# Unscaled exponentials in batch 0 and a scheduler whose ties are broken by random numbers, in an attention and channel-mixing kernel

## The chip, the core and the metric

The kernel runs on one core of one Trainium2 chip. The metric is the time of one execution in device microseconds (us). The engines are TensorE (PE in the profile; its weight loads are PEld), VectorE (DVE), ScalarE (ACT), GpSimd (POOL) and SyncE (SP), which issues nearly all DMAs. Each engine takes its instructions in the order in which the program wrote them for it, and they wait for each other by semaphores.

## The reference

Eight batches of 12 heads, 448 tokens, head size 64. Attention with an RMS norm of q and k, then a channel mix on its output:

```python
q_n, k_n = (rmsnorm(q, g_q), rmsnorm(k, g_k))
scores = scale * np.matmul(q_n, k_n.transpose(0, 1, 3, 2))
scores = scores - np.max(scores, axis=-1, keepdims=True)
attn = np.exp(scores)
attn = attn / (np.sum(attn, axis=-1, keepdims=True) + 1e-09)
out = np.matmul(attn, v)
...
xk = mu_k * x + (1.0 - mu_k) * x_prev
xr = mu_r * x + (1.0 - mu_r) * x_prev
k = np.maximum(xk @ w_k, 0.0)
v = k * k @ w_v
r = 1.0 / (1.0 + np.exp(-(xr @ w_r)))
return r * v
```

`x` is the attention's output with the heads side by side (768 columns), and `x_prev` the same, one token later. The three weights are float64 in the input (768 x 1024, 1024 x 768, 768 x 768).

## The kernel before

**Tiles.** Four heads of one batch are a quad `u` (24 in all, three to a batch), two heads a pair `i` (48, six to a batch). `load` fetches a quad's q and k, `stats` and `preps` normalise them, and `turn` or a transposing DMA brings them into the layout of the score products (`stk`). A quad has seven groups of score products (the list `groups`, line 824): three for the first pair, one shared by both pairs, three for the second. `scores` (826) issues a group's products into two PSUM banks; `expo` (864) reduces the row maximum on DVE and takes the exponential on ACT, which also sums the rows; `probs` (876) takes the probabilities further. `vload` and `vprep` (764) fetch and scale V; its small matmul of `vs` with the identity finds the maximum over partitions. `attends` (947) multiplies a pair's transposed probabilities (`pT`) with V into one PSUM bank `av` and copies it to the tile `x`. `mixk`, `mixr` and `mix` (1001) make xk and xr from `x`. `weights` (1037), `wscale` and `wsplit` turn the float64 weights into two f16 halves; a product of a weight tile with itself finds its column norms. `moe` (1144) does the products of a batch: eight tiles of xk with `wk`, and then, for each block of tokens and each half of the columns, xr with `wr` (1193) and the squared result `kk` with `wv`. Every product in f16 halves is three matmuls, so a batch has 144 matmuls xk with wk, 126 xr with wr and 168 kk with wv.

**Batch 0 is different.** Its three quads (`u < U32`, `U32 = 3`) work in float32. Their probabilities aren't transposed by a DMA, as in the other batches, but on PE, in `probs_pe` (909): two small DVE instructions make the scaled reciprocals of the row sums, two POOL passes multiply the exponentials by them (128x448 each), then seven transposes by the identity go to PSUM, and ACT or DVE copies them to `pT`. Ahead of 130 us PE also does the preparation of the weights, and much of the time it multiplies identity by identity in bf16: fillers, of which below.

**What sets the order.** Each of these functions is a thread that yields operations; the class `Plan` keeps a modelled clock for each engine and decides which thread's next operation is written next. `run` (365) computes for each thread the time at which its operation could start (the later of its engine's clock and the end of what it reads), takes off a tenth of the thread's priority, and takes the least (line 380):

```python
k = max(self.clk[th[2][0].eng] + wait, th[3] + slack) - PS * (th[1]() if callable(th[1]) else th[1])
```

`emit` (292) writes the operation behind the last one of its engine (so every instruction of the trace has its line, 298) and moves the modelled clock on, for PE by a cost in the operation's `form`: 130 ns a transpose (`TR_COST`), 110 ns a matmul of the weights' norms. Where the model sees PE idle by more than 200 ns ahead of an operation of certain kinds, `warm` (350) puts in fillers, 57 ns each, for 80% of that gap. So the number of fillers at a place tells how long a gap the planner foresaw there.

**The banks.** Eight PSUM banks go round among the users; `attends` and `vprep` share two of them (`OT_SHARE`).

Of the kernel before, what the change touches and what calls it, by code (L numbers as in the profile page):

```python
# [1 line left out]

# [14 lines left out]
P = 128  # L17
HD = 64
# [61 lines left out]
V_POOL = True  # L80
PE_T = 6
AHEAD = 0
U32 = 3
# [12 lines left out]
SC_KEEP = 1  # L96
TR_COST = 130
W_GAP = 6e3
# [122 lines left out]


WARM = ("tr", "sc", "t6", "av", "moe")
WARM_GAP = 200
# [5 lines left out]
class Plan:  # L230
    LAT = 35

    def __init__(self, tc):
        self.tc = tc
        self.clk = dict.fromkeys(("PE", "DVE", "ACT", "POOL", "SP"), 0.0)
        self.last, self.use, self.threads = {}, {}, []
        self.form, self.dma_free, self.acc, self.n = None, {"SP": 0.0, "ACT": 0.0}, False, 0
        self.held = {"DVE": [], "POOL": []}
        self.filler, self.own, self.bank, self.awake, self.warm_at = None, None, {}, False, 0.0

    def margin(self, form):
# [12 lines left out]
    def spawn(self, gen, prio=0):  # L254
        th = [gen, prio, None, 0.0]
        self.threads.append(th)
        self.advance(th)
# [14 lines left out]
    def advance(self, th):  # L272
        try:
            x = next(th[0])
        except StopIteration:
            self.threads.remove(th)
            return
        if isinstance(x, Op):
            x = [x]
        th[2] = x  # L280
        th[3] = self.ready(x) if isinstance(x, list) else 0.0

# [82 lines left out]
    def run(self):  # L365
        while self.threads:
            best, key = None, None
            for th in list(self.threads):
# [9 lines left out]
                if self.acc and th[2][0].eng == "ACT" and th[2][0].kw.get("accum_out") is not None:  # L378
                    wait += ACC_GAP
                k = max(self.clk[th[2][0].eng] + wait, th[3] + slack) - PS * (th[1]() if callable(th[1]) else th[1])  # L380
                if best is None or k < key:
# [101 lines left out]
def attn_moe_kernel(tc, q, k, v, small_in, w_k, w_v, w_r, out):  # L483
# [41 lines left out]
    st = {"wdone": 0, "g": 0, "moe": 0, "vl": 0, "gm": False, "mus": False, "want": "xk", "sg": 0, "su": 0, "pu": 0, "vi": 0, "wkeys": 0, "kdone": 0, "zq": 0, "tq": 0, "lu": 0, "pz": 0}  # L525
    LD, SS, VF, VV, TQ, PT, BS, BSC, XT, XK, XKN, XR, CNT, OS, CARRY, FR = {}, {}, {}, {}, {}, {}, {}, {}, {}, {}, {}, {}, {}, {}, {}, {}

# [180 lines left out]
    def turn(w, X, n, u):  # L708
        for a0 in range(0, NT, 4):
# [5 lines left out]
            for a in range(m):  # L715
# [4 lines left out]
                ops.append(T.transpose(form=("tr", TR_COST), out=o, in_=w[:, a0 + a, :], identity=ident))  # L720
            ops[0].form = ("tr", TR_COST * m)
            yield ops
# [100 lines left out]

    groups = [(u, *g) for u in range(NQ) for g in ((0, 0), (0, 2), (0, 4), (0, NT - 1), (1, 0), (1, 2), (1, 4))]

# [38 lines left out]
    def expo(gi, j, both, sums, D, tp):  # L864
        sp = both[j]
        if tp is not None:
            yield V.tensor_reduce(out=sums[:, j:j + 1], in_=sp[:, 0:S], axis=AX.X, op=ALU.max, negate=True)
            yield A.activation(out=tp.bitcast(F32).rearrange("p a c -> p (a c)")[:, j * S:(j + 1) * S], in_=sp[:, 0:S], func=AF.Exp, bias=sums[:, j:j + 1], accum_out=sums[:, 4 + 2 * j:5 + 2 * j])
            banks["sc"].put(sp)
            D[j] = True  # L870
            return
        yield V.tensor_reduce(out=sums[:, j:j + 1], in_=sp[:, 0:S], axis=AX.X, op=ALU.max, negate=True)
        yield A.activation(out=sp[:, 0:S], in_=sp[:, 0:S], func=AF.Exp, bias=sums[:, j:j + 1], accum_out=both[0][:, S + j:S + j + 1])
        D[j] = True
# [34 lines left out]
    def probs_pe(u, x, t0, sums, tp):  # L909
        r = sums[:, 8:11:2]  # L910
        yield V.tensor_scalar(out=r, in0=sums[:, 4:7:2], scalar1=1e-9, scalar2=2.0 ** -15, op0=ALU.add, op1=ALU.mult)
        yield V.reciprocal(out=r, in_=r)
        tf = tp.bitcast(F32).rearrange("p a c -> p (a c)")
        for j in range(2):
            w = tf[:, j * S:(j + 1) * S]
            yield G_.tensor_scalar(out=w, in0=w, scalar1=r[:, j:j + 1], scalar2=0.0, op0=ALU.mult, op1=ALU.add)
        c0 = S - HD if t0 == NT - 1 else x * S + (t0 + x) * HD
        for a0 in range(0, NT, 4):
# [3 lines left out]
            st["zq"] -= 1  # L922
            yield [T.transpose(form=("tr", TR_COST * m), out=z[:, a * P:(a + 1) * P], in_=tf[:, (a0 + a) * P:(a0 + a + 1) * P], identity=ident) for a in range(m)]
            src = z[:, 0:m * P].rearrange("p (a c) -> p a c", c=P)
# [22 lines left out]
    def attends():  # L947
        for i in range(NPAIR):
# [3 lines left out]
            pT = PT.pop(i)  # L952
            av = yield from banks["ot"].get()
            ops = []
            passes = PASSES32 if vl is None else PASSES
# [15 lines left out]
            for lo, hi in ((0, NT),) if i % 2 == 0 else ((NT - 1, NT), (0, NT - 1)):  # L971
                o = 0 if i % 2 == 0 or lo else HD
                yield A.activation(out=x[:, 1 + lo:1 + hi, :].rearrange("p t c -> p (t c)"), in_=av[:, o:o + (hi - lo) * HD], func=AF.Copy, scale=1.0 if iv is None else iv)
            banks["ot"].put(av)
# [62 lines left out]
    def weights():  # L1037
        for nm, w, kt, c, ci in WT:
# [27 lines left out]
            w16 = f.bitcast(BF16).rearrange("p (i n two) -> p i n two", two=2, n=P)[:, :, :, 1]  # L1066
            yield [T.matmul(form=("w", 110 * kt), out=pg[:, c % nb * P:(c % nb + 1) * P], lhsT=w16[:, i, :], rhs=w16[:, i, :], start=(c == 0 and i == 0), stop=(last and i == kt - 1)) for i in range(kt)]
            plan.filler = None if last else T.matmul(form=("x", 0), out=pg[:, 3 * P:4 * P], lhsT=ident16, rhs=ident16, start=False, stop=False)
# [241 lines left out]
```

## Time and profile before

| what | value |
|---|---|
| median of 3 runs | 989.4 us (989.07 to 989.49) |
| the profiled execution, time | 990.39 us |
| the profiled execution, span from the first to the last instruction | 988.6 us |
| PE, DVE, ACT, POOL busy, share of the span | 94%, 67%, 79%, 68% |
| mean granted clock of PE | 0.984 |
| instructions | 18862 |

A row of a group of instructions reads: line, engine, operation, output<-inputs by the program's names, partitions x elements, count | busy time in us, mean duration of one in ns | idle time of the engine just before them, and what ended most of it. A row of the waits reads: engine, tile and line that waited <- engine, tile and line waited for: us in total, times, the longest. A row of the timeline reads: start in us, duration in us, engine, operation, and in brackets the idle time before it and what ended it. `nat`, `xk` and `natx` are buffers that hold a group's exponentials (`xk` is lent out for that in batch 0), `sums` the row sums, `ps` any PSUM bank, `ident` the identity.

### The profile page before, as it was taken

The numbers are of one execution on the slowest core, as the hardware profiler recorded it, in microseconds if no ns is written. First come the engines' busy times: TensorE is split into PE (matmuls) and PEld (weight loads), VectorE is DVE, ScalarE is ACT, GpSimd is POOL, SyncE is SP. The second block draws the span as 40 slices with busy tenths as digits, with TensorE's granted clock in tenths as the row PEclk, the third lists the DMA queues.
The fourth block names the chain that finished last, engine by engine and source line by source line (L and its number), as shares of the span: only waits on it lengthen the run. The fifth ranks groups of instructions, "written<-read, shape, count | busy, mean of one in ns | idle before, by whom it ended". The sixth has DMA issues, their size and how long they took to land. (4 is left out here: it accounts for less than half of the span.)

```text
span 988.6 us, 18862 instructions
## 1 busy us (share of the span) xinstructions
PE 926.8 (94%) x6408; PEld 494.9 (50%) x6408; DVE 663.1 (67%) x1815; ACT 781.6 (79%) x1741; POOL 676.5 (68%) x744
## 2 busy tenths in 40 slices
PE   6878789799898999989999999999999999999997
PEld 5545454455444555445445454445544555565564
DVE  7888976888675878758778888688867875011000
ACT  4788899788996899979999999999999977424200
POOL 2789799756797677877787765977798725525400
PEclk9999999799898999999999999999999999999999
DMA  6634584789957999789979999899986993100000
GB/s 245 195 111 155 181 218 98 146 173 206 211 117 168 203 225 214 150 168 221 188 163 190 237 187 235 168 187 198 235 178 138 204 202 78 22 17 33 1 32 32
DMA packets 357648, 156.43 MB, mean 158 GB/s; under 512 B 336432, under 2 KB 336560, under 8 KB 357552
## 3 DMA queue, kind: packets, MB, share of 16 engines
q1 hardware_dynamic: 357408, 154.78, 71.5%
q8 instruction: 50, 0.82, 0.3%
q10 hardware_dynamic: 144, 0.46, 0.1%
q14 instruction: 46, 0.38, 0.1%
HBM read 60.24 MB, written 11.01 MB: 72 GB/s over the span
## 5 line engine op out<-in xcount | busy, mean ns | idle before, releaser
L298 PE MATMUL ps<-wv,kk 128*128 128x384 f16 x1344 | 234.4, 326 | 3.8 <-POOL kk L298 1.9
L298 PE MATMUL ps<-xk,wk 128*128 128x448 f16 x1152 | 225.9, 353 | 1.7 <-DVE o L298 1.0
L298 ACT ACTIVATE ps<-ps,sums 128x448 f32<-128x448 f32 x294 | 187.1, 638 | 20.9 <-DVE sums L298 19.2
L298 DVE TENSOR_REDUCE sums<-ps 128x1 f32<-128x448 f32 x336 | 192.4, 616 | 13.2 <-PE ps L298 12.5
L298 PE MATMUL ps<-wr,xr 128*128 128x384 f16 x1008 | 181.8, 332 | 3.3 <-ACT x L298 2.8
L298 DVE SCALAR_TENSOR_TENSOR nat<-ps,sums,nat 128x448 f16<-128x448 f32 x240 | 157.6, 678 | 35.6 <-ACT nat L298 34.8
L298 ACT ACTIVATE nat<-ps,sums 128x448 f16<-128x448 f32 (+1 forms) x272 | 171.2, 673 | 12.4 <-DVE sums L298 6.1
L298 PEld LDWEIGHTS <-kk 128*128 128x128 f16 (+1 forms) x1350 | 128.0, 98 | 100.9 <-issue 17.4
L298 PEld LDWEIGHTS <-wk 128*128 128x128 f16 (+1 forms) x1194 | 112.8, 98 | 112.6 <-issue 14.6
L298 PE MATMUL ps<-stk 64*128 64x448 f16 (+3 forms) x1104 | 128.2, 377 | 14.8 <-DVE nat L298 4.1
L298 PEld LDWEIGHTS <-xr 128*128 128x128 f16 x1008 | 97.4, 99 | 77.8 <-issue 18.6
L298 DVE SCALAR_TENSOR_TENSOR o<-o,ps 128x384 f32<-128x384 f32 x56 | 30.7, 549 | 111.9 <-PE ps L298 111.9
L298 DVE SCALAR_TENSOR_TENSOR df<-x,bsc,ps 128x448 f32<-128x448 f32 x96 | 64.4, 676 | 56.6 <-ACT ps L298 47.0
L298 PE MATMUL ps<-pT,vh 128*64 128x448 f16 x588 | 94.3, 364 | 3.8 <-DMA pT<-natx 1.3
L298 ACT ACTIVATE o<-ps,bsc 128x384 f32<-128x384 f32 x48 | 29.4, 612 | 72.0 <-PE ps L298 72.0
L298 POOL TENSOR_TENSOR qk<-qk,ss 128x896 f32<-128x896 f32 x36 | 60.8, 1688 | 23.3 <-DVE ss L298 22.8
L298 PEld LDWEIGHTS <-stk 64*128 64x128 f16 x1008 | 35.2, 97 | 69.8 <-issue 43.8
L298 POOL TENSOR_SCALAR o<-o,bsc 128x768 f32<-128x768 f32 x24 | 21.7, 905 | 67.7 <-DVE o L298 52.6
L298 POOL TENSOR_TENSOR xr<-df,xr 128x448 f16<-128x448 f32 x48 | 49.4, 1037 | 25.9 <-ACT xr L298 25.7
L298 POOL TENSOR_SCALAR vf<-vf,bstat 128x896 f32<-128x896 f32 x42 | 42.6, 1014 | 33.7 <-DVE bstat L298 28.7
L298 ACT ACTIVATE ps<-x,bsc 128x448 f32<-128x448 f32 x96 | 63.2, 668 | 2.1 <-POOL bsc L298 1.8
L298 POOL TENSOR_TENSOR xk<-df,xk 128x448 f16<-128x448 f32 x48 | 49.6, 1036 | 21.6 <-ACT xk L298 21.4
(174 smaller groups left out, 1576.6 us busy)
## 6 DMA issues: line engine op xcount, KB each, us to landing
vf<-in_v_dram SPq DMA_DIRECT2D x42, 448.0 KB, 4.2
out_dram<-o SPq DMA_DIRECT2D x28, 384.0 KB, 3.1
qk<-in_k_dram SPq DMA_DIRECT2D x23, 448.0 KB, 4.5
qk<-in_q_dram SPq DMA_DIRECT2D x22, 448.0 KB, 4.4
raw<-in_moe_w_v_dram SPq DMA_DIRECT2D x12, 512.0 KB, 4.3
raw<-in_moe_w_r_dram SPq DMA_DIRECT2D x12, 384.0 KB, 3.2
kk<-in_moe_w_k_dram SPq DMA_DIRECT2D x8, 384.0 KB, 5.1
raw<-in_moe_w_k_dram SPq DMA_DIRECT2D x8, 384.0 KB, 3.1
```

The source lines that it names most:

```text
L298: r = op.fn(op.kw["out"], op.kw["value"]) if op.fn.__name__ == "memset" else op.fn(**op.kw)
```

## The change

Three things are changed.

First, in batch 0 the exponentials are transposed unscaled. `expo` lets ACT put the row sums into a tile `acc` that is kept for the quad, 14 columns. `probs_pe` leaves out the two DVE instructions and the two POOL passes. In `attends` a pair's eight columns of `acc` become scaled reciprocals `rr` (two DVE instructions); the new function `spread_rows` multiplies each column, repeated 64 times, with the identity on PE, so that the reciprocals of all tokens stand in the bank `av` in the layout of the output (eight float32 matmuls); ACT copies them to `x`; then the products with V go into the same bank; and DVE multiplies `av` with the copied factors, where ACT copied `av` before.

Second, the planner's costs for transposes and for the weights' norms are others, and the spreading matmuls have a cost.

Third, `run` adds a random number to each candidate's key. It is drawn when the operation is made ready, is uniform between 0 and one of five amplitudes (3 to 200 ns of the modelled time), and its generator is seeded anew in each 15 us of the modelled time. The list `SEEDS` has one seed per stretch, 62 in all, 12 of them 0, which means no noise; a seed's remainder by 5 chooses the amplitude. The diff's core:

```diff
+PE_ROW = 125
...
-TR_COST = 130
+TR_COST = 109
...
+AMPS = [3.0, 10.0, 30.0, 80.0, 200.0]
+SEG = 15e3
...
+        self.seg = -1
+
+    def noise(self):
+        g = int(self.now() / SEG)
+        seed = SEEDS[g] if g < len(SEEDS) else 0
+        if g != self.seg:
+            self.seg, self.rng = g, Random(seed)
+        return AMPS[seed % 5] * self.rng.random() if seed else 0.0
...
+        th[4] = self.noise()
...
-                k = max(self.clk[th[2][0].eng] + wait, th[3] + slack) - PS * (th[1]() if callable(th[1]) else th[1])
+                k = max(self.clk[th[2][0].eng] + wait, th[3] + slack) - PS * (th[1]() if callable(th[1]) else th[1]) + th[4]
...
-            ops[0].form = ("tr", TR_COST * m)
+            ops[0].form = ("tr", TR_COST * m + 45)
...
+    QUAD = ((0, 0), (0, 2), (0, 4), (0, NT - 1), (1, 0), (1, 2), (1, 4))
+    groups = [(u, *g) for u in range(NQ) for g in QUAD]
+
+    def spread_rows(pt, x, col):
+        ops = []
+        for g, (y, t0) in enumerate(QUAD):
+            if t0 == NT - 1:
+                rows, cols = slice(x * HD, (x + 1) * HD), slice(x * (S - HD), x * (S - HD) + HD)
+                cols = slice(0, HD) if x else slice(S - HD, S)
+            elif y == x:
+                rows, cols = slice(0, P), slice((t0 + x) * HD, (t0 + x + 2) * HD)
+            else:
+                continue
+            for h in range(2):
+                ops.append(T.matmul(form=("f", 0), out=pt[h * HD:(h + 1) * HD, cols], lhsT=col(g)[rows, h:h + 1].broadcast_to([rows.stop - rows.start, HD]), rhs=ident[rows, rows], start=True, stop=True))
+        ops[0].form = ("f", PE_ROW * len(ops))
+        return ops
...
+            u = groups[gi][0]
+            if u < U32:
+                if u not in AC:
+                    AC[u] = small.tile([P, 2 * NT], F32, name="acc", bufs=U32)
+                c = 2 * (gi % NT) + j
+                acc = AC[u][:, c:c + 1]
+            else:
+                acc = sums[:, 4 + 2 * j:5 + 2 * j]
             yield V.tensor_reduce(out=sums[:, j:j + 1], in_=sp[:, 0:S], axis=AX.X, op=ALU.max, negate=True)
-            yield A.activation(out=tp.bitcast(F32).rearrange("p a c -> p (a c)")[:, j * S:(j + 1) * S], in_=sp[:, 0:S], func=AF.Exp, bias=sums[:, j:j + 1], accum_out=sums[:, 4 + 2 * j:5 + 2 * j])
+            yield A.activation(out=tp.bitcast(F32).rearrange("p a c -> p (a c)")[:, j * S:(j + 1) * S], in_=sp[:, 0:S], func=AF.Exp, bias=sums[:, j:j + 1], accum_out=acc)
...
-        r = sums[:, 8:11:2]
-        yield V.tensor_scalar(out=r, in0=sums[:, 4:7:2], scalar1=1e-9, scalar2=2.0 ** -15, op0=ALU.add, op1=ALU.mult)
-        yield V.reciprocal(out=r, in_=r)
         tf = tp.bitcast(F32).rearrange("p a c -> p (a c)")
-        for j in range(2):
+        if u >= U32:
+            r = sums[:, 8:11:2]
+            yield V.tensor_scalar(out=r, in0=sums[:, 4:7:2], scalar1=1e-9, scalar2=2.0 ** -15, op0=ALU.add, op1=ALU.mult)
+            yield V.reciprocal(out=r, in_=r)
+        for j in range(2) if u >= U32 else ():
             w = tf[:, j * S:(j + 1) * S]
             yield G_.tensor_scalar(out=w, in0=w, scalar1=r[:, j:j + 1], scalar2=0.0, op0=ALU.mult, op1=ALU.add)
...
+            u = i // 2
+            xc = x[:, 1:, :].rearrange("p t c -> p (t c)")
+            if u < U32:
+                o = 6 * (i % 2)
+                rr = small.tile([P, 8], F32, name="rr", bufs=2)
+                yield V.tensor_scalar(out=rr, in0=AC[u][:, o:o + 8], scalar1=1e-9, scalar2=2.0 ** -15, op0=ALU.add, op1=ALU.mult)
+                yield V.reciprocal(out=rr, in_=rr)
+                yield spread_rows(av, i % 2, lambda g: rr[:, 2 * g - o:2 * g - o + 2])
+                yield A.copy(out=xc, in_=av[:, 0:S]) if i % 2 == 0 else A.copy(out=x[:, NT:, :], in_=av[:, 0:HD])
+                if i % 2:
+                    yield A.copy(out=x[:, 1:NT, :], in_=av[:, HD:S])
...
-                yield A.activation(out=x[:, 1 + lo:1 + hi, :].rearrange("p t c -> p (t c)"), in_=av[:, o:o + (hi - lo) * HD], func=AF.Copy, scale=1.0 if iv is None else iv)
+                if u < U32:
+                    xs = xc[:, lo * HD:hi * HD]
+                    yield V.tensor_tensor(out=xs, in0=av[:, o:o + (hi - lo) * HD], in1=xs, op=ALU.mult)
+                    continue
+                yield A.activation(out=x[:, 1 + lo:1 + hi, :].rearrange("p t c -> p (t c)"), in_=av[:, o:o + (hi - lo) * HD], func=AF.Copy, scale=iv)
...
-            yield [T.matmul(form=("w", 110 * kt), out=pg[:, c % nb * P:(c % nb + 1) * P], lhsT=w16[:, i, :], rhs=w16[:, i, :], start=(c == 0 and i == 0), stop=(last and i == kt - 1)) for i in range(kt)]
+            yield [T.matmul(form=("w", 57 * kt + 20), out=pg[:, c % nb * P:(c % nb + 1) * P], lhsT=w16[:, i, :], rhs=w16[:, i, :], start=(c == 0 and i == 0), stop=(last and i == kt - 1)) for i in range(kt)]
```

**How it moves instructions.** On PE, fillers ahead of the first product xk with wk go from 346 to 279; the last product with V of batch 0 and that first product are parted by 118 fillers before and 38 now. Three places follow, of the order before and of the one now. In the rows a number behind a name is a buffer's.

The first is POOL in batch 0, where the last tile of `wk` is decoded (`kk` and `wr` from `raw`) and the first is scaled by `WSC`, rows 52 to 57 of POOL before:

```order
L298 TENSOR_SCALAR kk_98<-raw_705 128x384
L298 TENSOR_TENSOR nat_822<-nat_822 128x14x32
L298 TENSOR_SCALAR kk_98<-raw_753 128x384
L298 TENSOR_SCALAR xk_99<-xk_99,sums_103 128x448 x2
L298 TENSOR_SCALAR wr<-raw_885 128x384
L298 TENSOR_SCALAR wk<-wk,WSC 128x768
```

The two passes with `sums` are a group's scaling. On POOL at the same place, rows 38 to 42, stands now:

```order
L314 TENSOR_SCALAR kk_98<-raw_728 128x384
L314 TENSOR_SCALAR kk_98<-raw_749 128x384
L314 TENSOR_TENSOR nat_956<-qk_520,ss 128x2x7x64
L314 TENSOR_SCALAR wr<-raw_882 128x384
L314 TENSOR_SCALAR wk<-wk,WSC 128x768
```

The scaling is gone, the place comes 15 rows earlier, and the normalising of a later quad (`qk` with `ss`) has come in between.

The second is ACT where the last pair of batch 0 is taken out of PSUM (`x_1574` before, `x_1543` now; `x` with `bsc` is the mix, `wr` a weight's split, `ps` from `raw` a weight's decoding). Before:

```order
L298 ACTIVATE ps_1584<-raw_1542 128x512
L298 ACTIVATE wr<-wr,WSC 128x768
L298 ACTIVATE x_1574<-ps_1575 128x64
L298 ACTIVATE x_1574<-ps_1575 128x384
L298 ACTIVATE ps_1611<-x_1270,bsc 128x448
```

Here the two rows of `x_1574` take the product with V out of its bank. On ACT now:

```order
L314 ACTIVATE ps_1538<-raw_1504 128x512
L314 COPY x_1543<-ps_1544 128x64
L314 ACTIVATE ps_1600<-x_1361,bsc 128x448
L314 COPY x_1543<-ps_1544 128x384
L314 ACTIVATE stk_1452<-ps_1587,gc 128x384
```

The two copies stand at nearly the same place (rows 155 and 156 of ACT before, 155 and 157 now), but before they took the product with V, and now they take the spread factors, with that product still to come.

The third is PE where batch 1 goes over from xk with wk to xr with wr. Before (the end of a product with V, then the small matmul of `vprep`, then the first of xr with wr):

```order
L298 LDWEIGHTS vh_3571
L298 MATMUL ps_3892<-pT,vh_3571 64x448
L298 LDWEIGHTS vs
L298 MATMUL ps_3994<-ident_75,vs 128x128
L298 LDWEIGHTS xr_1861
L298 MATMUL ps_4009<-wr,xr_1861 128x384
```

The matmul with `vs` stands ahead of the product with wr. On PE now (the end of two groups of score products, then the first of xr with wr):

```order
L314 MATMUL ps_3847<-stk_3165 64x448
L314 LDWEIGHTS stk_3165
L314 MATMUL ps_3846<-stk_3165 64x448
L314 LDWEIGHTS xr_1795
L314 MATMUL ps_3867<-wr,xr_1795 128x384
```

The small matmul with `vs` stands behind that product now, and behind the next one, kk with wv.

More of the change, by code (lines that the diff above doesn't have):

```diff
@@ L1 @@
 from contextlib import ExitStack, nullcontext
+from random import Random
 import concourse.bass as bass
@@ L220, in __getattr__ @@
         return lambda form=None, **kw: Op(self.name, f, {k: aps(x) if hasattr(x, "shape") else x for k, x in kw.items()}, form)
+SEEDS = [532085, 943229, 137441, 665259, 941472, 1001930, 45703, 463766, 40704, 648310, 663919, 63071, 391219, 26655, 380901, 392604, 1004959, 162311, 638232, 75530, 429841, 157162, 286846, 0, 401574, 778420, 810252, 427299, 0, 677766, 202085, 218035, 340892, 806227, 168295, 219649, 702761, 918481, 577434, 0, 397293, 0, 97245, 107330, 918208, 543066, 152518, 309653, 215923, 948643, 1032522, 312573, 0, 0, 0, 0, 201091, 0, 0, 0, 0, 72760]
+AMPS = [3.0, 10.0, 30.0, 80.0, 200.0]
+SEG = 15e3
 WARM = ("tr", "sc", "t6", "av", "moe")
@@ L254, in spawn @@
     def spawn(self, gen, prio=0):
-        th = [gen, prio, None, 0.0]
+        th = [gen, prio, None, 0.0, 0.0]
         self.threads.append(th)
@@ L525, in attn_moe_kernel @@
     st = {"wdone": 0, "g": 0, "moe": 0, "vl": 0, "gm": False, "mus": False, "want": "xk", "sg": 0, "su": 0, "pu": 0, "vi": 0, "wkeys": 0, "kdone": 0, "zq": 0, "tq": 0, "lu": 0, "pz": 0}
-    LD, SS, VF, VV, TQ, PT, BS, BSC, XT, XK, XKN, XR, CNT, OS, CARRY, FR = {}, {}, {}, {}, {}, {}, {}, {}, {}, {}, {}, {}, {}, {}, {}, {}
+    LD, SS, VF, VV, TQ, PT, BS, BSC, XT, XK, XKN, XR, CNT, OS, CARRY, FR, AC = {}, {}, {}, {}, {}, {}, {}, {}, {}, {}, {}, {}, {}, {}, {}, {}, {}
     plan.st = st
@@ L822, in batch_scales @@
         BSC[b] = sc
-    groups = [(u, *g) for u in range(NQ) for g in ((0, 0), (0, 2), (0, 4), (0, NT - 1), (1, 0), (1, 2), (1, 4))]
+    QUAD = ((0, 0), (0, 2), (0, 4), (0, NT - 1), (1, 0), (1, 2), (1, 4))
[14 more added lines that the diff above has]
+        return ops
     def scores():
@@ L922, in probs_pe @@
             st["zq"] -= 1
-            yield [T.transpose(form=("tr", TR_COST * m), out=z[:, a * P:(a + 1) * P], in_=tf[:, (a0 + a) * P:(a0 + a + 1) * P], identity=ident) for a in range(m)]
+            yield [T.transpose(form=("tr", TR_COST * m + 45), out=z[:, a * P:(a + 1) * P], in_=tf[:, (a0 + a) * P:(a0 + a + 1) * P], identity=ident) for a in range(m)]
             src = z[:, 0:m * P].rearrange("p (a c) -> p a c", c=P)
```

## The prediction

> **What bounds the kernel now.** I read the page first, then the windows of its stages, then the waits of TensorE (PE) and ScalarE (ACT), and last the timeline of PE where it waits longest. The page's head and first part:
>
> ```profile
> span 988.6 us, 18862 instructions
> ...
> PE 926.8 (94%) x6408; PEld 494.9 (50%) x6408; DVE 663.1 (67%) x1815; ACT 781.6 (79%) x1741; POOL 676.5 (68%) x744
> ```
>
> PE is busy for 94% of the span, so an average says "PE bound" and 62 us idle. Five windows say where those 62 us lie (the columns are the window's length, then the busy time of each engine, then the granted clock):
>
> ```profile
> core 0: us, PE busy (x) PEld busy (x) DVE busy (x) ACT busy (x) POOL busy (x), PEclk, DMA share, GB/s
> 0.00:120.00 120.00, 95.51 (x737) 57.67 (x739) 101.38 (x295) 88.99 (x204) 86.57 (x123) 0.97 0.54 175
> 120.00:186.00 66.00, 54.70 (x446) 31.02 (x443) 50.84 (x105) 62.56 (x130) 62.56 (x63) 0.95 0.64 153
> 186.00:320.00 134.00, 124.66 (x829) 64.12 (x828) 97.21 (x284) 113.02 (x256) 92.09 (x95) 0.94 0.88 178
> 320.00:800.00 480.00, 468.39 (x3282) 239.08 (x3282) 373.14 (x1045) 448.62 (x1019) 370.10 (x384) 1.00 0.95 194
> 800.00:988.60 188.60, 183.53 (x1124) 102.98 (x1120) 40.55 (x89) 68.42 (x137) 65.22 (x81) 1.00 0.18 44
> ```
>
> Up to 186 us PE is idle for 24.5 + 11.3 = 35.8 us; from 186 to 800 us for 9.3 + 11.6 = 20.9 us; behind 800 us only in the last 5 us. So the kernel has a front, in which batch 0 is computed and the weights are prepared, and a steady part, where PE has work nearly always. The first product with wr (line 1193, in `moe`) starts at 185.64 us. In both orders exactly 725 matmuls that are neither fillers nor the new spreading ones stand ahead of it, so whatever the front saves shows there and reaches the end, unless PE idles more later.
>
> What ends the front? From 120 to 186 us ACT is busy for 62.56 of 66 us, 95%: ACT is the bound there, and its work up to the last weight split is nearly the same in both orders (253 instructions before it in the old one, 257 in the new). Only idle time of ACT ahead of 120 us, 120 - 88.99 = 31.0 us, can be given back. Its waits in that window that the change can touch are those for transposes on PE and for sums on VectorE (DVE):
>
> ```profile
> ACT pT L298 <- PE ps L298: 4.8, 8, 1.0
> ...
> ACT nat L298 <- DVE sums L298: 2.4, 6, 0.7
> ACT xk L298 <- DVE sums L298: 1.9, 2, 1.1
> ```
>
> Together 9.1 us. On PE, in the first 200 us, the scaling on GpSimd (POOL) that is taken out is waited for by name:
>
> ```profile
> PE ps L298 <- POOL nat L298: 3.1, 6, 0.8
> ...
> PE ps L298 <- POOL xk L298: 1.6, 3, 0.8
> ```
>
> **What is removed.** The groups of the removed instructions, and DVE's reciprocal:
>
> ```profile
> L298 DVE RECIPROCAL sums<-sums 128x2 f32<-128x2 f32 x168 | 26.8, 161 | 2.6
> ...
> L298 POOL TENSOR_SCALAR nat<-nat,sums 128x448 f32<-128x448 f32 x32 | 21.9, 690 | 2.5 <-DVE sums L298 1.1 <-DVE bsc L298 0.3 <-ACT nat L298 0.2
> ...
> L298 DVE TENSOR_SCALAR sums<-sums 128x2 f32<-128x2 f32 x21 | 8.0, 386 | 2.1 <-ACT nat L298 1.8 <-ACT xk L298 0.3
> ...
> L298 POOL TENSOR_SCALAR xk<-xk,sums 128x448 f32<-128x448 f32 x10 | 7.0, 714 | 4.2 <-ACT nat L298 2.0 <-DVE sums L298 1.9
> ```
>
> POOL loses 21.9 + 7.0 = 28.9 us, DVE 8.0 + 21 x 0.161 = 11.4 us. Neither engine is full ahead of 120 us (86.57 and 101.38 of 120), so these sums are no gain by themselves. The gain is the path: a group's transposes wait no longer for two DVE instructions and two POOL passes, 0.386 + 0.161 + 2 x 0.69 = 1.9 us. It is worth part of the 9.1 us above, and the 4.7 us that PE waited for POOL lie in that same path and are not counted again.
>
> **What is added.** Each of the six pairs of batch 0 gets a scaled reciprocal of eight columns, eight spreading matmuls, ACT copies of the spread factors, and DVE products. The nearest rows are the transposes by the same identity, and a DVE instruction that reads PSUM with one SBUF tensor:
>
> ```profile
> L298 PE MATMUL ps<-ident,nat 128*128 128x128 f32 x189 | 30.2, 286 | 10.5 <-DVE nat L298 3.4 <-POOL nat L298 3.1 <-DVE kk L298 1.2
> ...
> L298 DVE SCALAR_TENSOR_TENSOR df<-x,bsc,ps 128x448 f32<-128x448 f32 x96 | 64.4, 676 | 56.6 <-ACT ps L298 47.0 <-POOL xr L298 8.6 <-POOL xk L298 0.6
> ```
>
> PE: 48 matmuls, not shown before. Pipelined they cost 30.2 / 189 = 0.16 us each, 7.7 us; alone 0.286 us, 13.7 us. They come in runs of eight, so I take 7.7. They lie in the front, where PE idles for 35.8 us, so they cost nothing while that cover lasts. DVE: 12 small instructions at 0.161 and six products at 0.676, half of them cut in two (I add 0.3 for each cut): 1.9 + 4.1 + 0.9 = 6.9 us, less than the 11.4 removed. ACT: nine copies out take the place of nine scaled copies of the same sizes, 0. The path of one pair grows: factors, spreading, copy, and only then the product with V, since they share one PSUM bank. I put that at 8 x 0.16 + 0.676 = 2.0 us; for the last pair it runs beside the last transposes, which also need PE and a copy out. Its bounds are 0 and +2.0 us.
>
> **Where the front ends.** The timeline of PE around the last product with V of batch 0 and the first product of the MoE:
>
> ```profile
> 115.73 4.22 PE L298 MATMUL ps<-pT,vf 128*64 128x448 f32 x16
> ...
> 121.03 1.95 PE L298 MATMUL ps<-ident 128*128 128x128 bf16 x32
> ...
> 125.59 4.35 PE L298 MATMUL ps<-ident 128*128 128x128 bf16 x75
> 130.37 0.40 PE L298 MATMUL ps<-wv 128*128 128x128 bf16 x4 [0.42 <-DVE wv L298]
> 132.19 0.41 PE L298 MATMUL ps<-wv 128*128 128x128 bf16 x4 [1.42 <-DVE wv L298]
> 132.44 3.57 PE L298 MATMUL ps<-xk,wk 128*128 128x448 f16 x18
> ```
>
> From 119.95 to 132.44 us, 12.5 us, PE does next to nothing that is needed. 118 fillers stand there; in the new order 38. A filler is 4.35 / 75 = 0.058 us, so 80 fewer are 4.6 us of foreseen gap. But the new order then plans a gap it did not have: 52 fillers, 3.0 us, between the last xk product and the first product with wr, where the old one has 7. There the trace shows real waits:
>
> ```profile
> 173.42 0.74 PE L298 MATMUL ps<-stk 64*128 64x448 f16 x6 [1.53 <-DVE nat L298]
> ...
> 175.68 1.26 PE L298 MATMUL ps<-stk 64*64 64x448 f16 x12 [1.51 <-ACT kf L298]
> 178.56 0.91 PE L298 MATMUL ps<-ident 128*128 128x128 bf16 x7 [1.62 <-DVE nat L298]
> ...
> 185.64 1.73 PE L298 MATMUL ps<-wr,xr 128*128 128x384 f16 x6 [2.40 <-ACT x L298]
> ```
>
> These 7.1 us follow from ACT being full, and stay. So I take the front's gain at 4 us: a little under half of the 9.1, near the 4.6 of the fillers. Bounds: the whole 9.1, and a loss of 2.0 by the last pair's path.
>
> **The steady part.** The noise reorders everything behind it too. The two longest waits of PE there are both in the preparation of V:
>
> ```profile
> 255.04 1.30 PE L298 MATMUL ps<-stk 64*128 64x448 f16 x6 [2.84 <-DVE bstat L298]
> ```
>
> ```profile
> 303.57 0.29 PE L298 MATMUL ps<-ident,vs 128*128 128x128 bf16 x1 [3.93 <-ACT vh L298]
> ```
>
> Around both the clock falls:
>
> ```profile
> 250.00:260.00 10.00, 7.16 (x48) 3.31 (x48) 8.11 (x22) 9.97 (x25) 8.47 (x8) 0.72 0.93 190
> ...
> 300.00:310.00 10.00, 6.43 (x25) 3.25 (x26) 3.99 (x11) 7.08 (x15) 10.00 (x8) 0.66 1.09 227
> ```
>
> The slowed work costs 0.28 x 7.16 = 2.0 and 0.34 x 6.43 = 2.2 us, so the two places are worth 2.84 + 3.93 + 2.0 + 2.2 = 11.0 us. The planner saw neither: the old order has no filler there. At the second, one small matmul for V stood ahead of a ready product with wr; in the new order it stands behind that product and the next one. But other small waits can appear, so I take a third, 3.7 us; bounds are all 11.0, and nothing.
>
> The Trainium skill (TensorE: Matmul & The Clock Gate, What's actually happening) says that the clock halves only after an idle window of about 3.4 us. By that rule the wait of 2.84 us would cost no clock; the row of 250 us shows 0.72 there, so the measurement decides. By the rule alone only 3.93 + 2.2 = 6.1 us would be at stake, a third of it 2.0, and the time 983 us.
>
> **The sum.** -4 - 3.7 = -7.7 us on the span of 988.6 us: 980.9. The profiled execution took 990.39 us, 1.8 more than its span, and becomes 982.7; the median of the three runs is 989.4, 1.0 lower, and becomes 981.7. I say 982.
>
> **The rivals.**
> *More.* All named waits of the front go (9.1) and both stalls (11.0): 989.4 - 20.1 = 969 us. For it: the waits are short and many, as a better order removes them. Against: ACT at 95% from 120 to 186 us. Chance 0.16.
>
> *No change.* The front is ACT's work up to the last weight split, which stays, and the earlier start of the MoE is waited off at the 52 planned fillers; in the steady part stalls move and do not go, since what the planner does not see it cannot search away. 989.4 us, within 2. Chance 0.13. That the noise only shuffles, and so does not do what a search is for, is this rival too.
>
> *Slower.* The new order brings each batch's MoE forward and lets attention fall behind. Score matmuls ahead of the first product of batches 1, 4, 5 and 6, counted in the orders: 240, 738, 882 and 1050 before, 222, 708, 852 and 1026 now. 30 of them are five groups, whose exponentials and splits are still owed by ACT:
>
> ```profile
> L298 ACT ACTIVATE ps<-ps,sums 128x448 f32<-128x448 f32 x294 | 187.1, 638 | 20.9 <-DVE sums L298 19.2
> ...
> L298 ACT ACTIVATE nat<-ps,sums 128x448 f16<-128x448 f32 (+1 forms) x272 | 171.2, 673 | 12.4 <-DVE sums L298 6.1
> ```
>
> That is 5 x 2 x (0.638 + 0.673) = 13.1 us of ACT, which is at 448.62 of 480 us, 93%, there. If PE waits for all of it and the front gives its 4, the time is 989.4 + 13.1 - 4 = 998 us. It decides from where the debt is larger than the products that PE has in hand; for it speaks ACT's load, against it that the products of batch 6 cover the last pairs. Chance 0.16.
>
> **How the numbers follow.** Forecast 0.55. The forecast's own range goes from 975 (both terms at about twice) to 987. The range takes in half of the rival "more" and the lower half of "slower": 970 to 992. 0.2% is 2.0 us, about what a measurement can tell here. Faster is the forecast and "more", 0.71; the same is "no change", 0.13; slower 0.16.
>
> **What would show it.** Right: no wait for a POOL scaling in the front; fewer idle us of ACT ahead of 120; the first product with wr near 181.5 us instead of 185.64; idle of PE between there and 800 us near 17 instead of 20.9 us and no window at a clock of 0.7. Wrong: a first product with wr at 185 us or later (the front gave nothing), or PE waiting for exponentials and splits at the starts of batches 4 to 6 (the debt of ACT).

## The result, and the profile after

The changed kernel takes 957.58 us (median of 4 runs, 957.28 to 959.41) against 989.24 us (4 runs): a ratio of 0.969, 95% interval 0.9669 to 0.9712. It is faster by 31.7 us, four times the forecast of 7.7 and past the low end of the range, 970. The profiled execution took 959.41 us.

The page's head, and the same five windows as before the change (the last ends with the span):

```profile
span 957.6 us, 18867 instructions
...
PE 918.4 (96%) x6494; PEld 503.0 (53%) x6494; DVE 663.0 (69%) x1795; ACT 783.8 (82%) x1740; POOL 649.3 (68%) x702
```

```profile
0.00:120.00 120.00, 105.45 (x911) 69.28 (x911) 104.18 (x284) 96.05 (x219) 69.37 (x90) 0.97 0.57 188
120.00:186.00 66.00, 60.31 (x451) 33.37 (x451) 51.78 (x126) 62.68 (x134) 59.89 (x60) 1.00 0.72 155
186.00:320.00 134.00, 127.92 (x897) 66.36 (x895) 103.80 (x291) 122.74 (x275) 98.37 (x101) 0.99 0.91 187
320.00:800.00 480.00, 472.24 (x3327) 247.60 (x3325) 374.55 (x1039) 448.33 (x1009) 363.51 (x384) 1.00 0.95 194
800.00:957.60 157.60, 152.50 (x915) 86.39 (x913) 28.66 (x59) 53.99 (x108) 58.20 (x71) 0.99 0.14 35
```

Look at the second window: ACT is busy for 62.68 of 66 us, as before (62.56), and the work is 16 us further on all the same. The timeline of PE has the three places by which the time is divided below:

```profile
121.01 0.40 PE L314 MATMUL ps<-wv 128*128 128x128 bf16 x4 [0.97 <-DVE wv L314]
...
122.78 1.48 PE L314 MATMUL ps<-xk,wk 128*128 128x448 f16 x7
...
161.39 3.08 PE L314 MATMUL ps<-ident 128*128 128x128 bf16 x52
...
169.64 1.62 PE L314 MATMUL ps<-wr,xr 128*128 128x384 f16 x9 [1.10 <-ACT x L314]
...
277.34 1.96 PE L314 MATMUL ps<-wr,xr 128*128 128x384 f16 x11
```

The first product xk with wk starts at 122.78 us (132.44 before), the first with wr at 169.64 (185.64), the first with wr of batch 1 at 277.34 (303.65). So of the 31.0 us by which the span is shorter, 9.7 + 6.3 + 10.3 = 26.3 are there by 277 us, and 4.7 come in the seven batches behind.

The waits of the front (up to 120 us) that the prediction named:

```profile
ACT nat L314 <- DVE sums L314: 6.8, 6, 2.9
ACT pT L314 <- PE ps L314: 1.4, 3, 0.8
ACT xk L314 <- DVE sums L314: 0.8, 1, 0.8
PE ps L314 <- POOL xk L314: 0.8, 2, 0.4
```

PE's waits for POOL fall from 4.7 to 0.8 us. ACT's three rows do not shrink: they were 9.1 us together and are 9.0, since the waits for transposes fall from 4.8 to 1.4 and those for sums rise from 2.4 + 1.9 = 4.3 to 7.6. ACT idles for 24.0 of the 120 us all the same (31.0 before), by waits that the prediction did not count.

The work that was added, from the groups of instructions:

```profile
L314 PE MATMUL ps<-ident,rr 128*64 128x128 f32 x72 | 5.2, 281 | 0.5 <-DVE rr L314 0.5
...
L314 DVE TENSOR_SCALAR rr<-acc 128x8 f32<-128x8 f32 x6 | 3.0, 500 | 0.0
L314 PE MATMUL ps<-ident,rr 64*64 64x64 f32 x24 | 2.0, 241 | 0.1
L314 DVE TENSOR_TENSOR x<-ps,x 128x448 f32<-128x448 f32 x3 | 1.9, 617 | 0.0
```

Spreading costs PE 7.2 us (each float32 matmul has two records), and PE waited 0.5 us for the factors.

Over the whole span PE is busy for 8.4 us less (926.8 before, 918.4 now) and idle for 22.6 us less (61.8 and 39.2).

### The profile page after: what moved, and what is told of

It is laid out like the page before. It is cut to its first block, busy times and chain, and to the rows that moved or that the text cites. A ratio compares the mean times of both kernels' runs of the same rounds, so it can differ in the third digit from the quotient of the medians.

```text
span 957.6 us, 18867 instructions
## 1 busy us (share of the span) xinstructions
PE 918.4 (96%) x6494; PEld 503.0 (53%) x6494; DVE 663.0 (69%) x1795; ACT 783.8 (82%) x1740; POOL 649.3 (68%) x702
## 5 line engine op out<-in xcount | busy, mean ns | idle before, releaser
L314 ACT ACTIVATE ps<-ps,sums 128x448 f32<-128x448 f32 x294 | 182.6, 624 | 27.8 <-DVE sums L314 24.5
L314 DVE TENSOR_REDUCE sums<-ps 128x1 f32<-128x448 f32 x336 | 191.5, 613 | 19.1 <-PE ps L314 15.5
L314 PE MATMUL ps<-wr,xr 128*128 128x384 f16 x1008 | 176.8, 326 | 1.5 <-ACT x L314 1.1
L314 PE MATMUL ps<-stk 64*128 64x448 f16 (+3 forms) x1104 | 123.9, 372 | 7.3 <-DVE nat L314 3.0
L314 PE MATMUL ps<-pT,vh 128*64 128x448 f16 x588 | 92.2, 356 | 4.6 <-DMA pT<-nat 2.6
L314 POOL TENSOR_TENSOR nat<-qk,nat 128x896 f16<-128x896 f32 x31 | 58.5, 1886 | 16.2 <-ACT nat L314 16.1
L314 POOL TENSOR_TENSOR nat<-nat 128x448 f32<-128x448 f32 x37 | 42.7, 1155 | 30.4 <-ACT nat L314 25.4
```

The costliest lines, as they stand in the source:

```text
L314: r = op.fn(op.kw["out"], op.kw["value"]) if op.fn.__name__ == "memset" else op.fn(**op.kw)
```

## The experiments

Three parts were changed at once, so the first four kernels part them: theory A says that the searched order gains, B that the unscaled exponentials do, C that the planner's corrected costs do. The table has every run, each ratio against runs of the kernel before that were taken with it (medians 989.24 to 990.04 us); its four columns behind the ratio are from the starts of PE's products in the timelines (us): to the first xk with wk; from there to the first wr; from there to the first wr of batch 1; from there to the end of the span.

| kernel | median us | ratio to before, 95% | xk | to wr | to wr of batch 1 | to the end |
|---|---|---|---|---|---|---|
| before | 989.24 | 1 | 132.4 | 53.2 | 118.0 | 685.0 |
| after | 957.58 | 0.9669 to 0.9712 | 122.8 | 46.9 | 107.7 | 680.3 |
| e1_no_noise | 978.36 | 0.9881 to 0.991 | 131.5 | 50.8 | 108.6 | 685.9 |
| e2_unscaled_alone | 977.8 | 0.9878 to 0.9907 | 132.3 | 45.3 | 111.3 | 687.3 |
| e3_costs_alone | 988.21 | 0.998 to 1.0008 | 144.0 | 51.6 | 107.3 | 686.6 |
| e4_other_seeds | 1024.26 | 1.0347 to 1.0382 | 138.4 | 40.8 | 147.0 | 696.2 |
| e5_other_seeds2 | 1009.24 | 1.0165 to 1.0229 | 138.1 | 53.3 | 111.0 | 704.2 |
| e6_front_seeds | 967.78 | 0.9747 to 0.98 | 121.8 | 46.8 | 107.0 | 689.1 |
| e7_late_seeds | 999.96 | 1.007 to 1.0128 | 131.1 | 51.2 | 116.8 | 700.4 |
| e8_passes_back | 968.27 | 0.9752 to 0.9805 | 132.8 | 47.8 | 107.9 | 679.8 |
| e10_drop_in_place | 980.18 | 0.9869 to 0.9932 | 126.1 | 53.2 | 115.3 | 684.3 |
| e11_load_only | 966.54 | 0.9728 to 0.9801 | 132.3 | 47.5 | 106.3 | 679.6 |
| e12_fill_two | 989.48 | 0.9981 to 1.0018 | 134.3 | 55.5 | 116.3 | 683.6 |
| e13_no_fillers | 963.44 | 0.9702 to 0.9764 | 127.1 | 49.3 | 106.3 | 679.4 |

### The three parts one by one

No noise (all seeds 0, all else as after):

```diff
-SEEDS = [532085, 943229, 137441, ...
+SEEDS = [0, 0, 0, ...
```

> The changed kernel with all 62 seeds 0, so that ties fall as before; unscaled exponentials and new planner costs stay. Theory A (the searched order is what gains): at least half of the 31.7 us goes, 975 to 990 us. Theory B (the unscaled exponentials shorten the front, and the order is a by-product): 957 to 968 us. First product with wr: A 178 to 186 us, B 168 to 173 us.

978.36 us, in theory A's range.

The unscaled exponentials alone (before's costs, no noise):

```diff
-TR_COST = 109
+TR_COST = 130
...
-            ops[0].form = ("tr", TR_COST * m + 45)
+            ops[0].form = ("tr", TR_COST * m)
...
-            yield [T.matmul(form=("w", 57 * kt + 20), out=pg[:, c % nb * P:(c % nb + 1) * P], lhsT=w16[:, i, :], rhs=w16[:, i, :], start=(c == 0 and i == 0), stop=(last and i == kt - 1)) for i in range(kt)]
+            yield [T.matmul(form=("w", 110 * kt), out=pg[:, c % nb * P:(c % nb + 1) * P], lhsT=w16[:, i, :], rhs=w16[:, i, :], start=(c == 0 and i == 0), stop=(last and i == kt - 1)) for i in range(kt)]
```

> The kernel before with unscaled exponentials in batch 0 alone: the planner's old costs, no noise. Theory A: 978 to 990 us, a gain of at most 10 us. Theory B: 957 to 970 us. A third theory C, that the corrected costs of transposes and weight norms matter most, expects 980 to 990 us here and 960 to 970 us in the run without noise.

977.8 us, 0.2 below theory A's range and far above B's: a gain of some 11.5 us. None of it is there at xk, which starts at 132.3 us for 132.4; it comes behind. The kernel before with the new costs alone (the same lines the other way):

> The kernel before with the planner's new costs alone: scaled exponentials, no noise. Theories A and B: 984 to 996 us, no gain that counts. Theory C: 970 to 980 us.

988.21 us; its interval takes in 1, so no change is shown. C falls. The row of this kernel in the table warns against reading one milestone: xk starts 11.6 us later than before, and all of it is made good by the first wr of batch 1, since attention had run ahead meanwhile (the trace has 126 records of score matmuls ahead of xk, 114 before).

The kernel after with other seeds (5 added to each that isn't 0, so its amplitude is the same):

```diff
-SEEDS = [532085, 943229, 137441, ...
+SEEDS = [532090, 943234, 137446, ...
```

> The changed kernel with every seed that is not 0 raised by 5: the same amplitudes in the same stretches, other random numbers. Theory A: noise that was not searched gains nothing, the same as without noise or worse, 975 to 995 us. Theory B: 957 to 970 us, as any order does.

1024.26 us, slower than either theory expected. With 10 added:

> The kernel after with a second set of seeds that nothing was found for (each seed that isn't 0 raised by 10, so that its amplitude stays). Theory A (noise of itself costs, above all behind the front; it pays only where it was searched): 995 to 1045 us, with the rest behind the first product with wr at 815 to 850 us. Rival (the first other set was an unlucky one): 960 to 985 us, about as without noise.

1009.24 us. So the unscaled exponentials bring some 11.5 us; random tie-breaking that nothing was searched for costs 31 to 46 us against no noise (978.36); the seeds that were found gain 20.8 us on it. A and B both hold, A with about two thirds. How the list `SEEDS` was found is not on record; that it was chosen by its result is inferred from these losses.

Where does noise cost? In e5 most of it lies behind the first wr of batch 1 (704.2 us against 685.9 without noise), in e4 between the first wr of batch 0 and that of batch 1 (147.0 us against 108.6). That window of e4, and PE's waits in it:

```profile
179.21:326.20 146.99, 131.17 (x1017) 71.51 (x1018) 107.28 (x294) 122.59 (x278) 92.81 (x98) 0.92 0.83 172
```

```profile
PE ps L314 <- DVE nat L314: 12.8, 7, 4.9
PE ps L314 <- DVE df L314: 5.7, 3, 3.9
```

No engine but PE is over 122.59 of 147 us, ACT idles for 24.4, and PE waits for DVE's work on `nat` and `df`. On the average of this window no engine is full, which points to the sequence; it is not shown, and which of its moves does it was not tried.

### Do seeds hold outside the run in which they were found?

Found seeds in the first 12 stretches only, 0 behind them; and the other way round:

```diff
-SEEDS = [532085, ... 663919, 63071, 391219, 26655, ...
+SEEDS = [532085, ... 663919, 63071, 0, 0, ...
```

> The kernel after with the found seeds kept in the first 12 stretches only (180 us of the planner's time), 0 behind them. Theory A (the search gains in the front and in the steady part, each with its own seeds): the first product with wr starts near 169.6 us as in the kernel after, and the rest takes about the 794.5 us that it took without any noise: 965.5 us. Rival (the search only gains by the front, the rest follows): near 958. Rival (the gain lies behind the front): near 978, as with no noise at all.

967.78 us, near the 965.5 of theory A: the three front columns are those of after (121.8, 46.8, 107.0), the rest takes 689.1 us, near the 685.9 without noise and 8.8 more than after.

```diff
-SEEDS = [532085, ... 663919, 63071, 391219, 26655, ...
+SEEDS = [0, ... 0, 0, 391219, 26655, ...
```

> The kernel after with the found seeds in stretches 12 to 61 only, 0 in the first 12. Theory A1 (a seed is good only for the state of the planner in which it was found; elsewhere it is a random draw like any other): the late seeds act as unsearched noise, the front ends near 182 us as without noise, the rest takes 815 to 843 us, so 1000 to 1025 us. Rival A2 (a seed's order is good of itself): the rest takes the 788 us of the kernel after, so about 972 us.

999.96 us, at the low end of A1's range: A1 holds. The very seeds that save 8.8 us behind the front in the kernel after cost 14.5 us there (700.4 against 685.9) when the state that they start from is another, and 8.2 between the first wr of batch 0 and that of batch 1 (116.8 against 108.6). They are no better there than seeds that nobody looked for (696.2 and 704.2 in e4 and e5).

### What the scaling cost: its load or its path?

The kernel after with the order of every other instruction held, and the 42 passes put back on POOL, unseen by the planner; the small DVE instructions stay out:

```diff
+        if u < U32:
+            for j in range(2):
+                w = tf[:, j * S:(j + 1) * S]
+                with tc.issue_after(plan.last["POOL"].ins):
+                    plan.last["POOL"] = nc.gpsimd.tensor_scalar(out=w, in0=w, scalar1=1.0, scalar2=0.0, op0=ALU.mult, op1=ALU.add)
```

> The kernel after, every engine's order held, with the 42 scaling passes of batch 0 put back on POOL (multiplying by 1 in place, not seen by the planner; the two small DVE instructions of a group stay out). Theory P (the passes cost by POOL's load and by the path to the transposes): 42 x 0.69 = 29 us more of POOL in a front where POOL has about 38 us idle; the first product with wr goes from 169.6 to 177 or later, the time to 965 to 972 us. Rival O (only the order counts, POOL and the path have slack): first product with wr within 1.5 us of 169.6, 957 to 960 us.

968.27 us: P holds, the passes cost 10.7 us, and xk starts at 132.8, where it started before the change. Then the same passes on a scratch buffer, filled once with 1.0, so that no transpose waits for them:

```diff
-                w = tf[:, j * S:(j + 1) * S]
+                w = HOME["kk"].rearrange("p a b c -> p (a b c)")[:, 6144:6144 + 2 * S].bitcast(F32)
```

> The kernel after, every engine's order held, with the 42 passes put back on POOL at the same places as in e8_passes_back, but on a scratch buffer that nobody waits for: POOL's load without the path. Theory Load (the other POOL work of the front, decoding and splitting of the weights, is pushed back and ends the front): first product xk with wk near 130 us, 965 to 968 us, like e8. Rival Path (POOL had slack, the wait of a group's transposes is what costs): first product xk with wk within 2 us of the 122.8 of the kernel after, 957 to 960 us.

966.54 us, xk at 132.3: it is the load. The load costs 9.5 us at xk, the passes' path 0.5 on top of it (1.7 by the medians, whose intervals overlap), which is within what a single profile can tell here (some 2 us, see the end). How can an engine that idles for 50 of 123 us lose 9.5 by 24 us of work (95.82 us of POOL up to xk for 72.15)? By its queue. The timeline of POOL in after, three of the decodings of the weights' bytes:

```profile
65.14 0.54 POOL L314 TENSOR_SCALAR wr<-raw 128x384 int32<-128x384 uint8 x1
...
77.17 0.56 POOL L314 TENSOR_SCALAR wr<-raw 128x384 int32<-128x384 uint8 x1
...
93.24 0.55 POOL L314 TENSOR_SCALAR wf<-raw 128x384 int32<-128x384 uint8 x1 [2.09 <-DMA raw<-in_moe_w_r_dram]
```

and the same three with the load:

```profile
68.71 0.53 POOL L314 TENSOR_SCALAR wr<-raw 128x384 int32<-128x384 uint8 x1
...
81.94 0.55 POOL L314 TENSOR_SCALAR wr<-raw 128x384 int32<-128x384 uint8 x1
...
101.01 0.53 POOL L314 TENSOR_SCALAR wf<-raw 128x384 int32<-128x384 uint8 x1 [2.17 <-DMA raw<-in_moe_w_r_dram]
```

They are 3.6, 4.8 and 7.8 us late: the decodings and splits of the weights stand behind the passes in POOL's order, and the buffer `raw` of each comes free for the next load only when it is decoded. So the loads come later too: those issued at 75.38 and 90.20 us in after are issued at 78.98 and 97.93 with the load. POOL itself waits for loads later on (2.09 and 2.17 us at the third decoding), where that time can't be used. The window from 80 to 100 us is the fullest one: POOL was busy there for 19.06 of 20 us in the kernel before, is for 11.50 in after, and for 17.42 with the load put back:

```profile
80.00:100.00 20.00, 17.36 (x138) 9.99 (x135) 16.63 (x36) 15.21 (x35) 19.06 (x26) 1.00 0.47 142
```

```profile
80.00:100.00 20.00, 18.15 (x154) 10.15 (x156) 18.59 (x55) 17.47 (x43) 11.50 (x17) 1.00 0.56 178
```

```profile
80.00:100.00 20.00, 15.71 (x123) 9.12 (x122) 15.50 (x34) 15.47 (x36) 17.42 (x25) 0.93 0.48 157
```

But no window of 20 us is full with the load put back, and half of the delay, 4.8 us, is there before 80 us. The delay builds up pass by pass along the queue, not in one full slice.

The reverse, on the kernel before with its order held: the passes and the two small DVE instructions are counted by the planner, but marked and not issued (the normalisation of batch 0 is so left out of the computation):

```diff
-        for op in (self.warm(ops[0], s) if e == "PE" else []) + ops:
+        for op in [] if getattr(ops[0], "skip", False) else (self.warm(ops[0], s) if e == "PE" else []) + ops:
```

> The kernel before, every engine's order held, with the 42 passes on POOL and the 42 small DVE instructions of batch 0 that make their factors left out (the planner still counts them; the row sums of batch 0 then scale nothing, so its normalisation is left out of the computation). Theory P: named waits of PE for POOL in the front (4.7 us) go and ACT's for PE shrink; the first product with wr from 185.6 to 179 or earlier, 980 to 983 us. Rival O (the gain of the unscaled exponentials is that the planner can order otherwise): within 2 us of 989.4.

980.18 us, in theory P's range: xk comes 6.4 us earlier, the next column is the same to the tenth (53.2), and both stalls of the steady part stay, with waits of 2.84 and 3.83 us:

```profile
247.26 1.13 PE L303 MATMUL ps<-stk 64*128 64x448 f16 x6 [2.84 <-DVE bstat L303]
```

```profile
294.47 0.23 PE L303 MATMUL ps<-ident,vs 128*128 128x128 bf16 x1 [3.83 <-ACT vh L303]
```

So the removed work is worth 6.4 to 10 us at xk with no order changed; in these two orders the stretch from xk to wr and the stalls do not depend on it.

That holds for a held order. Where the planner ordered anew without the passes and without noise (e1 and e2), xk starts at 131.5 and 132.3 us, about as in before. There, as in before, 32 of the 40 matmuls for the norms of `wv` stand ahead of xk; in after it is 24. So xk is back near its old place with the load put back in the found order (e11), and also with the load gone in an order that was not searched (e1); its 9.7 us can't be divided between the two.

### The clock

Fillers in two waits of the kernel before, ahead of the first product with wr and of the small matmul with `vs` that waits at 303.57 us:

```diff
+MORE = {157: 30, 265: 50}
...
+        more = []
+        if e == "PE":
+            more = [self.own(self.bank[ops[0].kw["out"].tensor.name])] * MORE.get(self.npe, 0)
+            self.npe += 1
-        for op in (self.warm(ops[0], s) if e == "PE" else []) + ops:
+        for op in more + (self.warm(ops[0], s) if e == "PE" else []) + ops:
```

> The kernel before, every engine's order held, with fillers put ahead of two waiting matmuls of PE: 30 ahead of the first product with wr (185.64 us, where PE waits 2.40) and 50 ahead of the small matmul with vs that waits 3.93 us at 303.57. The waits stay, PE is kept busy in them. Theory Clock (of the 15 us of the steady part some 5 are work at a lowered clock: 1008 matmuls of xr with wr take 181.8 us before and 176.8 after): the granted clock of 180 to 190 and 300 to 310 us rises from 0.70 and 0.66 to 0.9 or more, products with wr fall to about 178, 984 to 986 us. Rival (the lowered clock is only another sign of the idle time and costs nothing by itself): 988 to 990 us.

989.48 us, no change (10 runs of it, 13 of before). At the first place the fillers write the bank that the product writes, and they waited for ACT like the product itself (2.12 us, up to 187.47). The product came 2.3 us behind them, at 189.78, so there they only delayed it, and the clock of 180 to 190 us stayed low (0.67). At the second place they ran in the wait. The 18 products right behind it, before and now:

```profile
303.65 5.69 PE L298 MATMUL ps<-wr,xr 128*128 128x384 f16 x18
```

```profile
306.08 3.09 PE L304 MATMUL ps<-wr,xr 128*128 128x384 f16 x18
```

The clock of 300 to 310 us rose from 0.66 to 1.00, and the products took 3.09 us instead of 5.69: 2.6 us less, as theory Clock said of the place. From there to the end it is 683.6 us instead of 685.0, so 1.4 of the 2.6 us are left in these two profiles. The total came out as the rival said, but it does not decide: the fillers of the first place had cost 2.3 us on the way.

The kernel after without any filler, all else in the same order:

```diff
+        return []
         gap = s - begin - WARM_GAP
```

> The kernel after, every engine's order held, without its 350 fillers. Theory Clock: PE's needed work of the front (some 85 us to 122.8) is done at a lower granted clock, below 0.9 in the mean up to 120 us, and is late where others wait for it: first product with wr 3 to 10 us later, 961 to 968 us. Rival (PE has room in the front, and the fillers take room themselves): within 2 us of 957.6.

963.44 us, 5.9 more, in the range of theory Clock; but its mean clock up to 120 us is 0.97, as with the fillers, and not below 0.9. The clock falls only in places. Two windows of this run:

```profile
110.00:120.00 10.00, 7.09 (x36) 2.90 (x36) 7.20 (x15) 9.59 (x21) 9.47 (x10) 0.67 0.54 165
...
170.00:180.00 10.00, 8.90 (x58) 4.35 (x58) 7.46 (x17) 8.13 (x16) 8.46 (x8) 0.76 0.24 47
```

xk starts 4.4 us later and the next stretch is 2.4 longer. The fillers of after there, 52 of them ahead of the first wr product, look like a planned loss, but with them the stretch runs at a granted clock of 1.00, and without at 0.90.

## Why the prediction was wrong, point by point

**"Neither engine is full ahead of 120 us, so these sums are no gain by themselves. The gain is the path".** This is the step that failed in the front's term. The runs show the reverse: at xk the load of the passes is worth 9.5 us and their path 0.5, no more than the noise of a profile. POOL's 86.57 of 120 us said nothing of the weights' decodings that stood behind the passes in its queue. The size of the term hung on the 9.1 us of ACT's named waits, and these are still 9.0 us, so the gain did not come from there.

**"ACT is the bound there, and its work up to the last weight split is nearly the same"; only idle time of ACT ahead of 120 us can be given back.** Wrong as well: the 6.3 us from xk to wr came with ACT as busy as ever. The product doesn't wait for that split. ACT's timeline around it, before and after:

```profile
178.20 1.21 ACT L298 ACTIVATE wv<-wf,WSC 128x1024 f16<-128x1024 f32 x1
...
184.81 0.78 ACT L298 ACTIVATE x<-ps,bstat 128x64 f32<-128x64 f32 x2
```

```profile
169.01 0.58 ACT L314 ACTIVATE x<-ps,bstat 128x384 f32<-128x384 f32 x1
...
172.25 1.15 ACT L314 ACTIVATE wv<-wf,WSC 128x1024 f16<-128x1024 f32 x1
```

Both times the product starts 0.05 us behind the end of ACT's copy of `x` out of PSUM (185.59 and 169.59); the last split ends 6.2 us ahead of it before, and comes 2.6 us behind it now. A full engine bounds a place only by what it must do ahead of that place, and the order decides how much that is. "These 7.1 us follow from ACT being full, and stay" falls with it: by the prediction's own rows two of the four waits ended at DVE, and the stretch has taken 40.8 to 53.3 us in the orders without added fillers. The front's term was 4, at most 9.1, and measured 16.0; in the new order 9.5 to 10 of it go when the load comes back. That the front gained, as forecast, does not bear the reasoning out.

**The steady part, 3.7.** It measured 15.0. The two stalls of 11.0 us were the right places and are gone (PE's longest wait behind the first wr product is now 1.48 us), but a third of them was a guess with no row behind it. From the first wr of batch 0 to that of batch 1, where both lie, after takes 10.3 us less, and e1, e2 and e3, which nobody searched, 6.7 to 10.7 less, with PE idle for 5.8 to 6.7 us there instead of 9.4. The stalls belonged to that one order. The remaining 4.7 were not foreseen: they need the late seeds (without them 689.1 instead of 680.3 us).

The 10.3 us are not all stall, though. PE idles for 3.5 us less there and works for 6.9 less (108.66 and 101.81 us), also because attention has been put off: 144 score matmuls instead of 162. Behind the first wr product as a whole, with nearly the same number of matmuls (5231 and 5238), PE idles for 6.0 us less and is busy for 9.0 less. So the idle part of the two stalls (6.8) was a fair size without the third, and the busy time fell by more than the 4.2 us that were priced for the clock; 5.0 of the 9.0 are the products xr with wr (181.8 and 176.8 us), and what the rest is stays open.

**The clock's part, 2.0 + 2.2 of the 11.0.** The local price was about right (2.6 us at the second place for 2.2); what of it reaches the end is not settled (1.4 us between two profiles, nothing in the times, with the other fillers' delay in them). By the Trainium skill (TensorE: Matmul & The Clock Gate, What's actually happening) it takes an idle window of about 3.4 us to cool the clock, and by that the forecast would have been 983; the trace already spoke against it with 0.72 around an idle of 2.84 us. The same section puts the penalty of the first ramp at under 1% of a typical kernel's span; no run here has that ramp by itself, since e13 removes the fillers of every place (5.9 of 957.58 us, 0.6%).

**What was right.** The added work: 7.2 us on PE for 7.7 forecast, 8.3 on DVE (all of the factors and products) for 6.9, where the first of the two small instructions took 0.5 us each and not 0.161. No wait shows them as a cost beyond the 0.5 us above. Fewer idle us of ACT ahead of 120 (24.0 for 31.0), hardly a wait for POOL, PE idle for 14.9 us from the first wr product to 800 us (17 forecast), no window at a clock of 0.7 behind the front (the least is 0.87, at 240 us).

**The rivals.** "More" named the right places and is still 11 us short: it took the waits that had names for all that there was, and most of those of ACT did not go. "Slower" did not happen, but e4, e5 and e7 show that its outcome was near: the three orders with seeds that were not searched for their place end at 1000 to 1024 us. In e4 it was not a debt of ACT, which idles for 24.4 us in the stretch that lost most; e5 and e7 were not read for it. "The noise only shuffles" did not come about either: noise that was not searched lost 31 to 46 us.

What stays open: which single moves make the searched order's 20.8 us. The columns place them (8.7 ahead of xk, 3.9 up to wr, 0.9 up to the wr of batch 1, 5.6 behind, against e1; 19.1 of the spans), but no run took one move apart from the others.

## What to carry to other kernels

Ask of an engine not whether it is full on average, but whose work stands behind its instructions in its queue; to tell load from path, put the load back in a held order with nobody waiting for it. Before calling a busy engine the bound of a place, look at the instruction whose end releases the first product there, and count only what has to stand ahead of it. Here random tie-breaking lost time with both lists that nothing was searched for, and the found seeds of the later stretches were worth nothing once the front ahead of them had changed.

## What the runs showed of the hardware

A lowered clock is visible at once and small at the end here: 18 products took 5.69 us instead of 3.09, and all 350 fillers of the kernel after together are worth 5.9 us. And two executions of the same instructions differ in the front: e12, equal to before up to the first wr product, started xk at 134.3 us for 132.4, with a granted clock of 0.91 for 0.96 in the first 40 us. A single profile's milestone there is good to about 2 us.
